# A gated recurrence and a feed-forward block on one core: chunk steps get explicit places, and some work changes engines

## The chip, the core and the metric

The kernel runs on one core of a Trainium2 chip. A core has a matrix engine (TensorE, PE in the profile, with PEld for its weight loads), a vector engine (DVE), an activation engine (ScalarE, ACT), GpSimd (POOL) and a queue of DMA issues (SyncE, SP). Each engine works through its own instructions strictly in the order in which they stand; semaphores tell one engine that another is done. The metric is the device time of one execution in microseconds; less is better. All tensors that the engines work on are fp32; the two weight matrices arrive as fp64.

## The reference

```python
batch, n_heads, seq, head_dim = (4, 8, 768, 48)          # q, k, v, a_re, a_im
n_tokens, d_model, d_ff = (3072, 384, 2048)              # w_in (384, 2048), w_out (2048, 384)
mag = np.sqrt(a_re * a_re + a_im * a_im)
scale = np.minimum(mag, 0.999) / (mag + 1e-06)
a_re_n, a_im_n = (a_re * scale, a_im * scale)
for t in range(S):                                       # state S is complex, 48 x 48 per head
    new_re = ar * S_re - ai * S_im
    new_im = ar * S_im + ai * S_re
    S_re, S_im = (new_re + kv, new_im)                   # kv = k_t (outer) v_t
    y[:, :, t] = np.einsum('bhd,bhde->bhe', q[:, :, t], S_re)
x = y.transpose(0, 2, 1, 3).reshape(B * S, H * D)        # (3072, 384)
h = x @ w_in
sp = np.maximum(h, 0.0) + np.log1p(np.exp(-np.abs(h)))
out = (h * erf(sp)) @ w_out
```

## The kernel before

The 3072 tokens are cut into 12 units of 256 tokens (three to a batch), and a unit into two chunks of 128 tokens. For a unit the kernel does four things.

- **Gates** (`g_tan`, `g_turn`, `g_angle`, `g_sin`, `g_log`, `g_decay`): magnitude and angle of the gates, summed along the chunk by a product with a triangular matrix (tile `sum`). The angle is the arc tangent of ai/ar, and 1/ar is a DVE reciprocal (lines 734 and 735, tile `rec`) of a clamped ar; lines 743 and 745 clamp the squared magnitude (`s`) and the quotient (`th`). They end in factors `pr` and `CS`.
- **Chunk** (`chunk`, twice a unit): q and k are multiplied by the factors on DVE (`kr`, `qr`, `kt`, `qt`), transposed on PE (`tr`) and copied out of PSUM by ACT (`kT`, `qT`, line 846). The scores `sc` are masked on DVE into `A` (line 857), the chunk's k-v products `kv` update the state `S`, and `y` is built on PE from `A` and `S`. ACT copies it to `x` (line 890), PE transposes that (`xt`), ACT copies it to `xT` (line 899).
- **Input product** (`ff_in`, line 914): `h` = x @ w_in in two slabs of 1024 columns, 96 PE instructions a unit, copied out by ACT (line 916). `softplus` clamps h on DVE into `z` (line 930) and then runs Exp, Ln, Ln and Exp over the slab on ACT: `z` is the softplus, `yy` its reciprocal. `erf_times_h` takes a slab in four parts: GpSimd multiplies z by yy into `t` (line 948), ACT runs Gelu over z in place, and DVE combines them (lines 949, 951 and 952) in place into h.
- **Output product** (`ff_out`, line 966): h @ w_out, 64 PE instructions a unit, copied out by ACT to `o` (line 970) and stored.

The fp64 weights are read as integers and converted (`narrow`, lines 683 to 693) in 14 pieces, six of w_in and eight of w_out. A piece is four DVE instructions, a GpSimd one, two DVE, a GpSimd one, all over one buffer `words`, which shares the tag `z` (one buffer) with softplus: the pieces run strictly one after the other, and the first softplus waits for the last piece.

The main loop has 16 windows. Window w runs the chunks of unit w, the input product of unit w-1, the output product of unit w-2 and gates of units w+1 to w+3. Inside a window `weave` gives each stream of steps an interval, spreads its steps evenly over it and issues them by that place; the 22 chunk steps run evenly from 0 to 1. From the issued order and its own estimate of durations a scheduler then fixes the order on each engine. `act` groups the activations by table (three table sets), and a change of set costs a table load (line 638).

After the loop the kernel sums two collected quantities, compares each with a bound, and takes a second, slower way of computing (`product_path`) if a bound is exceeded.

## Time and profile before

| | |
|---|---|
| time, median of 3 runs | 985.98 us (983.36 to 987.53) |
| the profiled execution's own time | 981.68 us |
| its span, first to last instruction | 980.0 us |
| mean granted TensorE clock | 0.922 |
| PE busy | 812.8 us, 83% |
| DVE busy | 632.6 us, 65% |
| ACT busy | 579.6 us, 59% |
| POOL busy | 309.4 us, 32% |

Busy time is a sum over the whole span, so a share such as 83% mixes a beginning in which PE has little to do with a middle in which it hardly pauses; the windows of the section below take these stages apart. The granted clock is given as a share of 2.4 GHz. A fp32 product is recorded as two matmul instructions, so counts of line 914 and 966 are twice those of the program's order.

### The profile page before, as it was taken

How to read it: one execution, taken by the hardware profiler on the slowest of the kernel's cores; microseconds unless marked ns; L12 is line 12 of the kernel's file. 1: busy time of each engine (PE TensorE's matmuls, PEld its weight loads, DVE VectorE, ACT ScalarE, POOL GpSimd, SP SyncE). 2: the span in 40 equal slices, each digit the busy share in tenths (PEclk: the TensorE clock that was granted, in tenths of full speed). 3: DMA queues.
4: the chain of work that ended last, by engine and by line, in shares of the span. 5: the costliest groups of instructions: out<-in, count | busy, mean ns of one | idle time of the engine just before them, and what ended most of it. 6: DMA issues, size and time to landing. Idle time of an engine off the chain costs nothing. (4 is left out here: it accounts for less than half of the span.)

```text
span 980.0 us, 10235 instructions
## 1 busy us (share of the span) xinstructions
PE 812.8 (83%) x3882; PEld 618.2 (63%) x3882; DVE 632.6 (65%) x736; ACT 579.6 (59%) x737; POOL 309.4 (32%) x180
## 2 busy tenths in 40 slices
PE   0115788968849989999999898998999999999987
PEld 0004677755637767777767676776767786887654
DVE  6778987638687576865975965767647534664340
ACT  4515241236777777758568587677684766556650
POOL 3565443324342242431431423224302220132220
PEclk9998575888978989999999999999999899999989
DMA  7552333101030211120311211111011110000000
GB/s 171 133 151 71 86 81 97 49 0 33 2 77 19 34 33 33 33 49 18 65 33 23 43 33 34 33 33 33 7 27 34 33 33 1 17 1 17 1 16 20
DMA packets 148034, 41.77 MB, mean 43 GB/s; under 512 B 142068, under 2 KB 145160, under 8 KB 147208
## 3 DMA queue, kind: packets, MB, share of 16 engines
q1 hardware_dynamic: 147976, 41.03, 18.4%
q8 instruction: 32, 0.52, 0.2%
q14 instruction: 26, 0.21, 0.1%
HBM read 36.24 MB, written 4.75 MB: 42 GB/s over the span
## 5 line engine op out<-in xcount | busy, mean ns | idle before, releaser
L966 PE MATMUL ops<-w_out_sb,h 128*128 128x384 f32 x768 | 286.0, 512 | 16.6 <-DVE h L952 8.9
L914 PE MATMUL hps<-xT,w_in_sb 128*128 128x256 f32 x1152 | 267.8, 387 | 16.9 <-ACT h L916 14.6
L914 PEld LDWEIGHTS hps<-xT,w_in_sb 128*128 128x128 f32 x1152 | 220.3, 194 | 59.0 <-ACT h L916 15.9
L948 POOL TENSOR_TENSOR t<-z,yy 128x512 f32<-128x512 f32 x96 | 148.0, 1560 | 301.0 <-ACT yy L639 261.3
L639 ACT ACTIVATE z<-z 128x2048 f32<-128x2048 f32 (+1 forms) x144 | 152.2, 1057 | 119.9 <-POOL t L948 84.8
L966 PEld LDWEIGHTS ops<-w_out_sb,h 128*128 128x128 f32 x768 | 146.3, 200 | 99.7 <-issue 16.9
L949 DVE SCALAR_TENSOR_TENSOR yy<-t,yy 128x512 f32<-128x512 f32 x96 | 101.6, 1083 | 74.0 <-POOL t L948 74.0
L916 ACT COPY h<-hps 128x512 f32<-128x512 f32 x96 | 55.5, 581 | 86.1 <-PE hps L914 85.4
L951 DVE TENSOR_TENSOR z<-z,yy 128x512 f32<-128x512 f32 x96 | 88.0, 946 | 0.0
L882 PE MATMUL y<-v,A 128*128 128x48 f32 x384 | 77.2, 298 | 11.5 <-DVE A L857 11.5
L857 DVE TENSOR_TENSOR A<-sc,triu 128x512 f32<-128x512 f32 x48 | 32.7, 684 | 79.4 <-PE sc L854 79.4
L638 ACT ACT_TABLE_LOAD x64 | 82.1, 1283 | 1.1
L854 PEld LDWEIGHTS sc<-qT,kT 96*128 96x128 f32 x384 | 54.6, 214 | 44.5 <-ACT qT L846 40.3
L930 DVE TENSOR_SCALAR z<-h 128x1024 f32<-128x1024 f32 x48 | 42.2, 887 | 62.1 <-ACT h L916 59.9
L854 PE MATMUL sc<-qT,kT 96*128 96x128 f32 x384 | 61.0, 308 | 24.4 <-ACT qT L846 23.8
L765 PE MATMUL sum<-th,turns 128*128 128x384 f32 x48 | 26.4, 637 | 65.7 <-DVE th L762 50.6
L952 DVE SCALAR_TENSOR_TENSOR h<-z,h 128x512 f32<-128x512 f32 x96 | 78.4, 846 | 0.1
L882 PEld LDWEIGHTS y<-v,A 128*128 128x128 f32 x384 | 65.1, 216 | 16.1 <-DVE A L857 12.9
L885 PE MATMUL y<-S,qT 96*128 96x48 f32 x320 | 69.3, 302 | 0.0
L793 POOL TENSOR_TENSOR lr<-s,y 128x768 f32<-128x768 f32 x12 | 24.9, 2078 | 127.1 <-ACT y L639 97.0
L735 DVE RECIPROCAL rec<-rec 128x768 f32<-128x768 f32 x12 | 59.4, 4950 | 0.3
L885 PEld LDWEIGHTS y<-S,qT 96*128 96x128 f32 x320 | 56.0, 218 | 0.0
(80 smaller groups left out, 972.4 us busy)
## 6 DMA issues: line engine op xcount, KB each, us to landing
raw<-in_moe_w_in_dram SPq DMA_DIRECT2D x6, 1024.0 KB, 7.1
raw<-in_moe_w_out_dram SPq DMA_DIRECT2D x8, 768.0 KB
ar<-in_a_re_dram SPq DMA_DIRECT2D x24, 192.0 KB, 3.2
ai<-in_a_im_dram SPq DMA_DIRECT2D x24, 192.0 KB, 3.4
q<-in_q_dram SPq DMA_DIRECT2D x24, 192.0 KB, 3.6
k<-in_k_dram SPq DMA_DIRECT2D x24, 192.0 KB, 2.9
v<-in_v_dram SPq DMA_DIRECT2D x24, 192.0 KB, 3.8
out_dram<-o SPq DMA_DIRECT2D x24, 192.0 KB, 1.9
```

Of the source, the lines that this page charges most:

```text
L638: in_order(nc.scalar.preload_act_table_set(sets[0]))
L639: in_order(nc.scalar.activation(func=func, **kw))
L735: nc.vector.reciprocal(out=rec, in_=rec)
L854: nc.tensor.matmul(out=ps[:, j, :], lhsT=st["k", g][0:D2, j, :], rhs=st["q", g][0:D2, j, :], start=True, stop=True)
L882: nc.tensor.matmul(out=y[:, j, :], lhsT=st["A", g][:, i, :], rhs=T["v", u][:, c, j, :], start=True, stop=first)
L885: nc.tensor.matmul(out=y[:, j, :], lhsT=st["q", g][0:D2, i, :], rhs=T["S"][0:D2, j, :], start=False, stop=True)
L914: nc.tensor.matmul(out=ps[:, e, :], lhsT=w_in_sb[:, kd, f0:f0 + P], rhs=T["xT", u][:, kd, :], start=(kd == 0), stop=(kd == KD - 1))
L948: nc.gpsimd.tensor_tensor(out=t, in0=z, in1=y, op=OP.mult)
L949: nc.vector.scalar_tensor_tensor(out=y, in0=t, scalar=-2.0, in1=y, op0=OP.add, op1=OP.mult)
L951: nc.vector.tensor_tensor(out=z, in0=z, in1=y, op=OP.mult)
L952: nc.vector.scalar_tensor_tensor(out=h, in0=z, scalar=1.0 / RT2, in1=h, op0=OP.add, op1=OP.mult)
L966: nc.tensor.matmul(out=ps, lhsT=T["h", u, sl][:, e, jj * P:(jj + 1) * P], rhs=w_out_sb[:, i, :], start=(i == 0), stop=(i == KF - 1))
```

## The change

- The chunk steps get places of their own in a window: a list of (place, step) with the 11 steps of a chunk between 0.0 and 0.45 of its half of the window, `state` before the scores, and both `qT` copies ahead of them. All streams are put in one list `plan` and sorted. The gate steps of a unit move: `g_mag` and `g_log` of unit w+2, `g_angle`, `g_decay` and `g_sin` of unit w+1, where the angles were those of w+2 and the magnitudes those of w+3.
- The clamps and the reciprocal go. 1/ar becomes Ln and Exp on ACT (in `g_log`), the softplus reads h directly. In their place five sums are collected, partly as by-products of activations (`accum_out`), and compared with five bounds (`LIMITS`; the last is for the sum of the reciprocals `yy`) at the end.
- Gelu writes a buffer `e` of its own (two of them), where it wrote over z. The product t = z * yy goes from GpSimd to DVE.
- The copies `qT`, `x` and `o` go from ACT to DVE.

```diff
+LIMITS = (1e13, 0.0, 1e15, 1e18, 1e8)
...
-    def g_tan(u):
+    def g_mag(u):
...
-            act(out=m, in_=m, func=AF.Relu, accum_out=off[:, u:u + 1])
-            T["s"], T["y"] = s, y
+            T["s"], T["y"], T["m"] = s, y, m

         def s1():
-            rec = t_("rec")
-            nc.vector.tensor_scalar(out=rec, in0=ar, scalar1=2.0**-60, scalar2=None, op0=OP.max)
-            nc.vector.reciprocal(out=rec, in_=rec)
-            T["rec"] = rec
-
-        def s2():
-            rec = T["rec"]
-            nc.gpsimd.tensor_tensor(out=rec, in0=rec, in1=ai, op=OP.mult)
-
-            s = T["s"]
-            nc.vector.tensor_scalar(out=s, in0=s, scalar1=2.0**-63, scalar2=2.0**63, op0=OP.max, op1=OP.min)
-            th = gat.tile([P, C, DM], FP, tag="th", name="th")
-            nc.vector.tensor_scalar(out=th.rearrange("p c f -> p (c f)"), in0=rec, scalar1=SLOPE, scalar2=-SLOPE,
-                                    op0=OP.min, op1=OP.max)
-            T["th", u] = th
-        return [s0, s1, s2]
+            act(out=T["m"], in_=T["m"], func=AF.Relu, bias=LEAST, accum_out=off[:, u:u + 1])
+        return [s0, s1]
...
     def g_log(u):
...
+            act(out=m, in_=ar, func=AF.Ln)
+            act(out=m, in_=m, func=AF.Exp, scale=-1.0)
             act(out=s, in_=s, func=AF.Ln)
             act(out=y, in_=s, func=AF.Exp, scale=-0.5)
             act(out=y, in_=y, func=AF.Ln, scale=EPS, bias=1.0)
+            th = gat.tile([P, C, DM], FP, tag="th", name="th")
+            nc.gpsimd.tensor_tensor(out=th.rearrange("p c f -> p (c f)"), in0=m, in1=ai, op=OP.mult)
...
-                nc.scalar.copy(out=t[0:D2], in_=ps[0:D2])
+                (nc.scalar.copy if nm == "k" else nc.vector.tensor_copy)(out=t[0:D2], in_=ps[0:D2])
...
-            nc.scalar.copy(out=x, in_=y.rearrange("p h d -> p (h d)"))
+            nc.vector.tensor_copy(out=x, in_=y.rearrange("p h d -> p (h d)"))
...
-        return [prep("k", 1), prep("q", 0), cols("k", 0), cols("k", 1), cols("q", 0), scores(0), cols("q", 1),
-                scores(1), state, y_, xT]
+        return [(0.0, prep("k", 1)), (0.03, prep("q", 0)), (0.06, cols("k", 0)), (0.09, cols("k", 1)),
+                (0.12, cols("q", 0)), (0.15, cols("q", 1)), (0.2, state), (0.25, scores(0)), (0.28, scores(1)),
+                (0.36, y_), (0.45, xT)]
...
     def softplus(u, sl):
...
-            for i in range(0, SLAB, half):
-                nc.vector.tensor_scalar(out=z[:, i:i + half], in0=h[:, i:i + half], scalar1=8.0, scalar2=-16.0,
-                                        op0=OP.min, op1=OP.max)
-            act(out=z, in_=z, func=AF.Exp)
+            act(out=z, in_=T["h", u, sl], func=AF.Exp, accum_out=exps[:, i:i + 1])
...
-                nc.gpsimd.tensor_tensor(out=t, in0=z, in1=y, op=OP.mult)
+                e = yp.tile([P, n, NT], FP, tag="e", name="e", bufs=2)
+                act(out=e, in_=z, func=AF.Gelu, scale=RT2)
+                nc.vector.tensor_tensor(out=t, in0=z, in1=y, op=OP.mult)
                 nc.vector.scalar_tensor_tensor(out=y, in0=t, scalar=-2.0, in1=y, op0=OP.add, op1=OP.mult)
-                act(out=z, in_=z, func=AF.Gelu, scale=RT2)
-                nc.vector.tensor_tensor(out=z, in0=z, in1=y, op=OP.mult)
-                nc.vector.scalar_tensor_tensor(out=h, in0=z, scalar=1.0 / RT2, in1=h, op0=OP.add, op1=OP.mult)
+                nc.vector.tensor_tensor(out=e, in0=e, in1=y, op=OP.mult)
+                nc.vector.scalar_tensor_tensor(out=h, in0=e, scalar=1.0 / RT2, in1=h, op0=OP.add, op1=OP.mult)
...
-                    nc.scalar.mul(out=o, in_=ps, mul=-RT2)
+                    nc.vector.tensor_scalar(out=o, in0=ps, scalar1=-RT2, scalar2=None, op0=OP.mult)
...
-            (0.0, 1.0, rec),
...
-            (0.0, 0.45, f0), (0.45, 0.9, f1),
...
+            plan += [(0.5 * c + p, f) for c in range(C) for p, f in chunk(w, c)]
+        plan += at(0.0, 0.9, weights_in() if w == -1 else weights_out() if w == 0 else [])
+        plan += at(0.0, 1.0, only(w - 2, ff_out))
...
+        for _, f in sorted(plan, key=lambda e: e[0]):
+            f()
```

The first place is DVE in the beginning, where pieces of w_out are converted (`words`, `w_out_sb`) among the chunks of the second unit (numbers tell buffers apart). Line numbers after are those of the changed kernel. Before:

```order
L735 RECIPROCAL rec_960<-rec_960 128x768
L683 TENSOR_SCALAR words_440<-raw_439 128x768
L792 TENSOR_SCALAR s_552<-s_552 128x768
L684 TENSOR_SCALAR words_440<-words_440 128x768
L874 TENSOR_TENSOR Skv_855<-kv_845,S_664 96x384
L685 TENSOR_SCALAR words_440<-raw_439 128x768
L857 TENSOR_TENSOR A_810<-sc_805,triu_114 128x512
L687 SCALAR_TENSOR_TENSOR w_out_sb_128<-raw_439,words_440 128x768
L875 TENSOR_TENSOR S_854<-Skv_855,w_412 96x384
L857 TENSOR_TENSOR A_837<-sc_832,triu_114 128x512
```

After:

```order
L686 TENSOR_SCALAR words_433<-raw_432 128x768
L868 TENSOR_TENSOR S_742<-Skv_743,w_449 96x384
L687 TENSOR_SCALAR words_433<-words_433 128x768
L850 TENSOR_TENSOR A_759<-sc_754,triu_114 128x512
L688 TENSOR_SCALAR words_433<-raw_432 128x768
L850 TENSOR_TENSOR A_774<-sc_769,triu_114 128x512
L690 SCALAR_TENSOR_TENSOR w_out_sb_131<-raw_432,words_433 128x768
L883 COPY x_814<-y_797 128x384
L693 TENSOR_SCALAR words_433<-w_out_sb_131 128x768
```

The reciprocal is gone from between the conversion's instructions; the copy of `x`, which waits for PE's `y`, now stands between them.

The second place is DVE in a unit in the middle, at the second half of a slab's elementwise work (the same instructions for the first half stand just ahead). Before:

```order
L949 SCALAR_TENSOR_TENSOR yy<-t,yy 128x512 x2
L951 TENSOR_TENSOR z<-z,yy 128x512 x2
L952 SCALAR_TENSOR_TENSOR h<-z,h 128x512 x2
L762 SCALAR_TENSOR_TENSOR th<-row,th 1x384
L930 TENSOR_SCALAR z<-h 128x1024
L743 TENSOR_SCALAR s<-s 128x768
```

After:

```order
L937 TENSOR_TENSOR t<-z,yy 128x512 x2
L938 SCALAR_TENSOR_TENSOR yy<-t,yy 128x512 x2
L939 TENSOR_TENSOR e<-e,yy 128x512 x2
L940 SCALAR_TENSOR_TENSOR h<-e,h 128x512 x2
L824 TENSOR_TENSOR qr<-q,pr 128x384
L839 COPY qT<-tr 96x512 x2
L850 TENSOR_TENSOR A<-sc,triu 128x512 x2
L958 TENSOR_SCALAR o<-ops 128x384
```

Before, DVE went on with clamps and angles, since ACT made `qT`. Now the two `qT` copies of the second chunk stand in DVE's queue, behind the 16 elementwise instructions of a slab, of which four are the products `t`.

The third place is PE for the same chunk, from the transposes of q to `y`. Before:

```order
L843 MATMUL tr<-ident,qt 96x128 x4
L966 MATMUL ops<-w_out_sb,h 128x384 x4
L854 MATMUL sc<-qT,kT 128x128 x4
L843 MATMUL tr<-ident,qt 96x128 x4
L966 MATMUL ops<-w_out_sb,h 128x384 x2
L854 MATMUL sc<-qT,kT 128x128 x4
L966 MATMUL ops<-w_out_sb,h 128x384 x2
L866 MATMUL kv<-v,kt 96x48 x8
```

After:

```order
L908 MATMUL hps<-xT,w_in_sb 128x256 x6
L836 MATMUL tr<-ident,qt 96x128 x8
L908 MATMUL hps<-xT,w_in_sb 128x256 x6
L954 MATMUL ops<-w_out_sb,h 128x384 x4
L859 MATMUL kv<-v,kt 96x48 x8
L847 MATMUL sc<-qT,kT 128x128 x8
L954 MATMUL ops<-w_out_sb,h 128x384 x4
```

Between the transposes of q and the scores, which need the `qT` copies, there stood 4 and 2 output products; now there stand 6 input products, 4 output products and the 8 products `kv`.

## Rows read from the trace of the kernel before

**Rows 1.** The page: engines over the span; granted TensorE clock in 40 slices.
```profile
PE 812.8 (83%) x3882; PEld 618.2 (63%) x3882; DVE 632.6 (65%) x736; ACT 579.6 (59%) x737; POOL 309.4 (32%) x180
...
PEclk9998575888978989999999999999999899999989
```

**Rows 2.** Windows: stretch, length, then PE, PEld, DVE, ACT, POOL busy (count), clock, DMA.
```profile
0.00:212.00 212.00, 120.34 (x512) 96.38 (x512) 160.24 (x170) 70.01 (x109) 95.62 (x53) 0.82 0.38 97
212.00:314.00 102.00, 72.41 (x288) 51.72 (x289) 71.15 (x77) 73.92 (x84) 38.38 (x23) 0.80 0.16 31
314.00:902.00 588.00, 554.48 (x2862) 426.20 (x2862) 376.43 (x456) 405.31 (x514) 164.69 (x96) 0.98 0.14 29
902.00:980.00 78.00, 65.58 (x222) 43.88 (x222) 24.74 (x36) 30.38 (x31) 10.71 (x8) 0.91 0.04 14
```

**Rows 3.** Windows of line 914 alone: PE and PEld busy (count), clock, DMA.
```profile
314.00:902.00 588.00, 199.57 (x865) 162.82 (x866) 0.98 0.14 29
```

**Rows 4.** Windows, one late stretch (columns as in rows 2).
```profile
842.00:902.00 60.00, 59.47 (x313) 46.17 (x314) 32.66 (x45) 35.99 (x42) 12.74 (x8) 1.00 0.02 8
```

**Rows 5.** Waits of PE from 314 to 902 us: total, times, longest.
```profile
PE xt L898 <- ACT x L890: 11.2, 8, 2.7
PE sc L854 <- ACT qT L846: 8.4, 10, 1.7
```

**Rows 6.** Timeline (start us, us, instruction): first and last weight conversion begin, what follows.
```profile
31.57 0.68 DVE L683 TENSOR_SCALAR words<-raw 128x1024 uint32<-128x1024 uint32 x1
...
203.58 0.56 DVE L683 TENSOR_SCALAR words<-raw 128x768 uint32<-128x768 uint32 x1 [1.99 <-POOL w_out_sb L693]
...
211.78 1.29 DVE L930 TENSOR_SCALAR z<-h 128x1024 f32<-128x1024 f32 x2 [1.98 <-POOL w_out_sb L693]
```

**Rows 7.** Lines of DVE, 31.5 to 212 us: count | busy, mean ns | idle.
```profile
L735 DVE RECIPROCAL rec<-rec 128x768 f32<-128x768 f32 x3 | 14.8, 4944 | 0.0
...
L745 DVE TENSOR_SCALAR th<-rec 128x768 f32<-128x768 f32 x4 | 7.4, 1858 | 0.0
...
L743 DVE TENSOR_SCALAR s<-s 128x768 f32<-128x768 f32 x3 | 7.1, 2378 | 8.2 <-POOL s L726 8.2
```

**Rows 8.** Timeline: second A tile of a chunk, the copy of its y.
```profile
145.44 0.68 DVE L857 TENSOR_TENSOR A<-sc,triu 128x512 f32<-128x512 f32 x1
...
151.34 0.48 ACT L890 COPY x<-y 128x384 f32<-128x384 f32 x1 [9.75 <-PE y L885]
```

**Rows 9.** Lines over the whole span (columns as in rows 7).
```profile
L948 POOL TENSOR_TENSOR t<-z,yy 128x512 f32<-128x512 f32 x96 | 148.0, 1560 | 301.0 <-ACT yy L639 261.3 <-DVE Skv L874 24.6 <-DVE yy L949 15.1
...
L949 DVE SCALAR_TENSOR_TENSOR yy<-t,yy 128x512 f32<-128x512 f32 x96 | 101.6, 1083 | 74.0 <-POOL t L948 74.0
...
L638 ACT ACT_TABLE_LOAD x64 | 82.1, 1283 | 1.1
...
L639 ACT ACTIVATE yy<-z 128x2048 f32<-128x2048 f32 x24 | 45.9, 1911 | 0.3
L930 DVE TENSOR_SCALAR z<-h 128x1024 f32<-128x1024 f32 x48 | 42.2, 887 | 62.1 <-ACT h L916 59.9 <-POOL w_out_sb L693 2.0
...
L857 DVE TENSOR_TENSOR A<-sc,triu 128x512 f32<-128x512 f32 x48 | 32.7, 684 | 79.4 <-PE sc L854 79.4
...
L639 ACT ACTIVATE y<-s 128x768 f32<-128x768 f32 x12 | 10.2, 854 | 0.1
```

**Rows 10.** Lines of ACT by form: the Gelu.
```profile
L639 ACT ACTIVATE z<-z 128x512 f32<-128x512 f32 x96 | 60.5, 630 | 86.7 <-POOL t L948 84.8
```

**Rows 11.** Timeline: line 949 with no GpSimd work beside it.
```profile
289.68 0.68 DVE L949 SCALAR_TENSOR_TENSOR yy<-t,yy 128x512 f32<-128x512 f32 x1
```

**Rows 12.** Timeline of PE: input products back to back.
```profile
785.67 2.75 PE L914 MATMUL hps<-xT,w_in_sb 128*128 128x256 f32 x12
```

**Rows 13.** Timeline: the last two groups of output products.
```profile
935.79 10.48 PE L966 MATMUL ops<-w_out_sb,h 128*128 128x384 f32 x32
...
951.05 23.40 PE L966 MATMUL ops<-w_out_sb,h 128*128 128x384 f32 x64 [4.65 <-ACT o L970]
```

More of the change, by code (lines that the diff above doesn't have):

```diff
@@ L624, in quotient_path @@
     nc.vector.tensor_scalar(out=turns, in0=triu, scalar1=1.0 / TAU, scalar2=None, op0=OP.mult)
-    off = const.tile([P, NU], FP, name="off")
-    spans = const.tile([P, NU * C], FP, name="spans")
+    seen = [const.tile([P, n], FP, name=f"seen{i}") for i, n in enumerate((NU * C, NU, NU, NU * NSL, NU * NSL))]
+    spans, off, large, exps, inverse = seen
     w_in_sb = const.tile([P, KD, FF], FP, name="w_in_sb")
@@ L978, in only, with at @@
         return steps(u) if 0 <= u < NU else []
+    def at(begin, end, steps):
+        return [(begin + (end - begin) * (i + 0.5) / len(steps), f) for i, f in enumerate(steps)]
     load_gates(0)
-    load_gates(1)
     load_qkv(0)
-    for f in g_tan(0):
-        f()
     for w in range(-2, NU + 2):
-        load_gates(w + 4)
+        load_gates(w + 3)
         if w >= -1:
             load_qkv(w + 2)
-        rec = chunk(w, 0) + chunk(w, 1) if 0 <= w < NU else []
-        f0 = only(w - 1, lambda u: ff_in(u, 0) + softplus(u, 0) + erf_times_h(u, 0))
-        f1 = only(w - 1, lambda u: ff_in(u, 1) + softplus(u, 1) + erf_times_h(u, 1))
-        wts = weights_in() if w == -1 else weights_out() if w == 0 else []
-        weave(
-            (0.0, 1.0, rec),
-            (0.0, 0.05, only(w + 2, g_turn) + only(w + 1, g_sin)),
-            (0.0, 0.9, wts),
-            (0.0, 0.45, f0), (0.45, 0.9, f1),
-            (0.2, 1.0, only(w - 2, ff_out)),
-            (0.3, 0.7, only(w + 2, g_angle)),
-            (0.15, 0.151, only(w + 1, g_decay) + only(w + 2, g_log)),
-            (0.5, 0.8, only(w + 3, g_tan)),
-        )
@@ L1005, in quotient_path @@
-    total = const.tile([P, 2], FP, name="total")
-    nc.vector.tensor_reduce(out=total[:, 0:1], in_=spans, axis=mybir.AxisListType.X, op=OP.add)
-    nc.vector.tensor_reduce(out=total[:, 1:2], in_=off, axis=mybir.AxisListType.X, op=OP.add)
-    ps = ps_b.tile([P, 2], FP, tag="b", name="all")
-    nc.tensor.matmul(out=ps[0:1, :], lhsT=ones, rhs=total, start=True, stop=True)
-    both = const.tile([1, 2], FP, name="both")
-    nc.vector.tensor_scalar(out=both[:, 0:1], in0=ps[0:1, 0:1], scalar1=SPAN, scalar2=None, op0=OP.is_le)
@@ L1012, in quotient_path @@
-    nc.vector.tensor_scalar(out=both[:, 1:2], in0=ps[0:1, 1:2], scalar1=0.0, scalar2=None, op0=OP.is_le)
-    nc.vector.tensor_tensor(out=ok, in0=both[:, 0:1], in1=both[:, 1:2], op=OP.mult)
+        plan = []
+        if 0 <= w < NU:
+            plan += [(0.5 * c + p, f) for c in range(C) for p, f in chunk(w, c)]
+        plan += at(0.0, 0.9, weights_in() if w == -1 else weights_out() if w == 0 else [])
+        plan += at(0.0, 1.0, only(w - 2, ff_out))
+        if 0 <= w - 1 < NU:
+            for sl in range(NSL):
+                b = 0.06 + 0.4 * sl
+                plan += at(b, b + 0.24, ff_in(w - 1, sl))
+                plan += [(b + 0.25, softplus(w - 1, sl))]
+                plan += at(b + 0.3, b + 0.42, erf_times_h(w - 1, sl))
@@ new lines, in quotient_path @@
+        plan += at(0.05, 0.1, only(w + 2, g_mag))
+        plan += at(0.1, 0.45, only(w + 1, g_angle))
+        plan += at(0.3, 0.305, only(w + 1, g_decay))
+        plan += at(0.71, 0.711, only(w + 2, g_log))
+        plan += at(0.9, 0.95, only(w + 1, g_sin) + only(w + 2, g_turn))
+        for _, f in sorted(plan, key=lambda e: e[0]):
+            f()
+    n = len(seen)
+    sums = const.tile([P, n], FP, name="sums")
+    for i, t in enumerate(seen):
+        nc.vector.tensor_reduce(out=sums[:, i:i + 1], in_=t, axis=mybir.AxisListType.X, op=OP.add)
@@ L1016 @@
+    ps = ps_b.tile([P, n], FP, tag="b", name="all")
+    nc.tensor.matmul(out=ps[0:1, :], lhsT=ones, rhs=sums, start=True, stop=True)
+    within = const.tile([1, n], FP, name="within")
+    for i, limit in enumerate(LIMITS):
+        nc.vector.tensor_scalar(out=within[:, i:i + 1], in0=ps[0:1, i:i + 1], scalar1=limit, scalar2=None, op0=OP.is_le)
+    nc.vector.tensor_reduce(out=ok, in_=within, axis=mybir.AxisListType.X, op=OP.min)
 def kernel(
```

18 lines of the change are left out of this document (9 added, 9 removed).

## Prediction

> **What bounds the kernel now.** I read the page first. PE is busy 83% of the span, twenty per cent ahead of the next engine, but the line of its granted clock falls below full speed almost only in the first third [rows 1]. So one share for the whole span says little, and I cut the span into four stages by events of the program [rows 2]: to 212 us, where the last weight conversion ends; to 314, where the input product of the third unit begins; to 902, where that of the twelfth begins; and to the end. Line 914 alone has 865 instructions between 314 and 902, nine units of 96 [rows 3], so a unit takes 588 / 9 = 65.3 us there.
>
> In these nine units PE is busy 554.5 of 588 us at a clock of 0.98 [rows 2], and between 842 and 902, where the gates are all done and DVE, ACT and POOL have least to do, 59.5 of 60.0 us [rows 4]. That is PE's own pace: 60 us a unit. The 5.3 us above it are the price of being fed late; the waits that end last are copies by ACT, 11.2 us for `x` and 8.4 us for `qT` [rows 5].
>
> Before 212 us PE does 120 us of work at a clock of 0.82. The stage is set by the 14 weight conversions, which run from 31.57 to 211.78 us, one after the other over one buffer, alternating between DVE and POOL; directly behind the last stands the first clamp of softplus [rows 6]. The last piece, with nothing between its instructions, takes 211.78 - 203.58 = 8.2 us; the mean is 180.2 / 14 = 12.9. The rest is what stands in DVE's queue between them. From 212 to 314 PE is busy 72 of 102 us, since the first output product waits for the first slab's softplus and the third unit's chunks for ACT and DVE. After 902 it is busy 65.6 of 78 us [rows 2].
>
> **The change part by part.** Sums are made against the profiled execution: a span of 980.0 us and 1.7 us around it, 981.7, which is 4.3 us below the median of the three runs, 985.98.
>
> *Beginning.* Between the first and the last conversion DVE loses three reciprocals, 14.8 us, four clamps of the angle, 7.4 us, and three of the magnitude, 7.1 us: 29.3 us [rows 7]. It gains, for the four chunks of the first two units, eight `qT` copies and four `x` copies. DVE's copy out of PSUM is not in the trace; the nearest row is the mask `A`, which reads as many columns out of PSUM, 0.68 us, against 0.48 us for ACT's copy of `x` [rows 8]. I take 0.68: 12 x 0.68 = 8.2 us. And DVE now waits for PE: `x` stands one or two conversion instructions behind the second `A`. Before, from the end of that `A` (146.1) to the copy of `x` (151.3) 5.2 us passed [rows 8], of which the two conversion instructions between take about 1.2 [rows 6]. Three chunks (the very first has half the products and its `x` stands far behind) make 3 x 4 = 12 us. What is queued behind the waiting copy is the conversion itself, so this is on the path. Against that, four instructions of the third unit's first chunk (two of them `A`) now stand behind the last conversion: 4 x 0.7 = 3 us less. Sum: -29.3 + 8.2 + 12 - 3 = -12. Bounds: -29 if PE is always early, +6 if each `qT` also waits 2 us.
>
> *Filling up.* After the last conversion ACT sets the pace, since a slab's four passes take 4 x 1.91 = 7.6 us [rows 9]. Before, each slab also had clamps ahead of it and the Gelu wrote over z, so it had to wait for POOL's t: 84.8 us of waiting in all [rows 10]. Now a slab is 7.6 + two table loads of 1.28 + four Gelu of 0.63 + two copies of `h` at the Gelu's 0.6 + some 2.5 us for the two `e` buffers = 16.4 us; the second slab has five gate activations of 0.85 besides, 20.7. With Abs and Sin the third unit's factors are there 39 us after the last conversion. Its first chunk takes some 12 us; the second chunk's `qT` stands behind the next slab on DVE, whose Gelu ACT reaches 22 us later (about ten gate activations and four copies, then 7.6 and a load), at 61; DVE's 16 instructions at 0.68 [rows 11] end at 70, and `qT`, `A`, `y`, `x` and the transposes need 8 more. So the third unit's input product begins 78 to 80 us after the last conversion, instead of 102: -22. Bounds: -35, and 0 if DVE and ACT hold each other up as before.
>
> *The nine units.* PE's instructions stay the same, so 60 us is the floor. What fed it late changes: `qT` and `x` go to DVE; behind the transposes of q PE now has six input products, four output products and `kv` to do instead of two to four output products. DVE's load was 376 / 9 = 41.8 us a unit [rows 2]. It loses the reciprocal and its clamps (about 7 us), four softplus clamps of 0.89 and, with POOL's t gone, the stretching of line 949 from 0.68 [rows 11] to 1.08 [rows 9], eight times: -14. It gains eight t and eight copies at 0.68: +10.9. So some 39 of 60. ACT had 405 / 9 = 45 us; it loses eight copies of 0.48 [rows 8] and gains two gate activations of 0.85 and six read-outs of sums, which I bound by the same 0.85 each: 43 to 48. Both stay under PE, which hides the read-outs and the copies; if that cover goes, they cost their 5 us a unit. I take half of the excess as won: 9 x 1.8 = -16. Bounds: 9 x 5.3 = -48 by the late stretch [rows 4], and above zero by the rival below.
>
> *Tail.* Before, 32 output products ran after the last input product, then PE waited 4.65 us and ran 64 [rows 13]. Now 44 products of the program's order, 88 instructions, follow the last input product, and the last slab's softplus lies beside the first 56 of them: 56 x 0.33 = 18 us against 7.6 + 1.3 + 0.6 for ACT and 5.4 for half a slab on DVE. So the 4.65 us go, and of the slack in 23.4 - 64 x 0.33 = 2.3 us part: with the clamps (2 x 0.89) gone -10 is my value, for the stage as a whole has 12.4 us without PE. Bounds: -12 and +2, the latter for the five comparisons at the end, which now wait for the last product.
>
> Sum: -12 - 22 - 16 - 10 = -60. 981.7 - 60 = 921.7; with the 4.3 us to the median, 926.
>
> **The rivals.** *Copies behind the elementwise block (slower).* In the nine units and the two before, DVE works through 16 instructions of a slab ahead of the second chunk's `qT`. They take 16 x 0.68 = 10.9 us, or 17.3 at the mean of 1.08 [rows 9]. Behind the transposes PE has 12 instructions of 0.23 [rows 12], 8 of 0.33 [rows 13] and `kv`, about 6.7 us. If DVE begins the block only when PE comes to those transposes, PE waits 5 to 11 us a unit. From 5.5 us on, 11 units eat the 60 us; at 8 the time is 926 + 88 = 1014. For it: strict order, and the block itself waits for ACT's Gelu. Against it: DVE has 20 us a unit to spare, and PE comes to the transposes only after that slab's input products.
>
> *PE is the bound and only the beginning moves.* Units and tail stay as they are: 926 + 26 = 952; if the fill does not move either, 974. For it: PE's work is unchanged and its waits in rows 5 are only 20 us. Against it: the late stretch at 60.
>
> *PE is fed without a gap.* All of 48 and the fill's 35: 926 - 32 - 13 = 881.
>
> *Headroom in PE.* By the share of weight loads, 46.2 of 60 us in the late stretch [rows 4], a unit could come down to 46 us, and nine of them would be 174 us shorter than now: about 800. But 96 x 0.23 + 64 x 0.33 = 43 us of a unit are the two big products back to back [rows 12, 13], and the chunks' products come on top, so the trace speaks against it. The Trainium skill's page "Perfetto Trace Analysis", section "Identifying the Most-Contended Engine", calls matmul busy time a bad measure of how near PE is to its limit and asks for the weight loads' share instead; by that rule this case would hold, and the row disagrees.
>
> *The condition fails.* Then the second path runs as well, and the time far exceeds 1500. With the reference's inputs the sum of the reciprocals is 9.1e6 against a bound of 1e8, and the others are further off.
>
> **How the numbers follow.** My forecast, 900 to 948: 0.52. Only the beginning moves, 948 to 981: 0.19. PE without a gap, 870 to 900: 0.08. Headroom: 0.01. Nothing to be seen, 981 to 991: 0.06. Copies behind the block, above 991: 0.135. The condition: 0.005. The runs before lie within 0.4%, so 0.5% is what can be told from no change. Faster: 0.52 + 0.19 + 0.08 + 0.01 = 0.80; same 0.06; slower 0.14. The range 882 to 985 leaves out about 0.05 below and 0.17 above; the likeliest case's own is 900 to 948.
>
> **What would show it.** Right: the last conversion ends near 200 us, the third unit's input product begins near 280, nine units take about 571 us, and 68 follow; DVE's mean for the line of `yy` falls to about 0.7; PE's longest wait for a DVE copy stays under 3 us. Wrong: conversions that end after 212 with DVE waiting for PE ahead of `x`; waits of PE's scores for `qT` of over 5 us in every unit; or a unit that still takes 65 us with PE waiting for ACT's copies of `h`.

## The result and the profile after

The changed kernel takes 896.94 us (median of 4 runs, 895.91 to 899.13) against 984.67 us before (977.97 to 987.53): a ratio of 0.912, 95% interval 0.907 to 0.917. That is 88 us less, where 60 were forecast (926 us); the time lies inside the range of 882 to 985, and just below the likeliest case's own range of 900 to 948.

The page of the changed kernel, engines over the span of 894.5 us and the granted clock in 40 slices (answers to [rows 1]):

```profile
PE 780.3 (87%) x3882; PEld 605.7 (68%) x3882; DVE 549.8 (61%) x838; ACT 559.4 (63%) x725; POOL 154.8 (17%) x84
...
PEclk9655685689999999999999999999999999999999
```

POOL has lost half of its work and DVE 83 us, though DVE has 102 instructions more. The same four stages, cut at the events of [rows 2]: end of the last conversion (192.8), third unit's input product (269.7), twelfth unit's (828.6). Columns as there.

```profile
0.00:192.80 192.80, 103.88 (x460) 85.89 (x460) 111.67 (x152) 59.37 (x94) 88.18 (x50) 0.69 0.39 103
192.80:269.70 76.90, 66.91 (x314) 48.42 (x314) 51.82 (x79) 66.61 (x80) 7.68 (x5) 0.96 0.15 30
269.70:828.60 558.90, 551.69 (x2898) 431.52 (x2897) 362.59 (x562) 404.94 (x521) 58.95 (x30) 0.99 0.16 33
828.60:894.50 65.90, 57.83 (x213) 39.86 (x212) 23.73 (x47) 28.52 (x31) 0.00 (x0) 0.97 0.05 17
```

The beginning is 19 us shorter than before, the fill 25, the nine units 29, the tail 12. In the nine units PE was busy about as long as before (551.7 against 554.5 us); what shrank is the time in which it did nothing, from 588.0 - 554.5 = 33.5 us [rows 2] to 558.9 - 551.7 = 7.2. In the fill, too, 20 of the 25 us are such time (29.6 us before, 10.0 now); the other 5 are PE's busy time, at a granted clock of 0.96 where it had been 0.80. The waits of PE in the nine units (total, times, longest) are these, and the copies `x` and `qT` of [rows 5] are no longer among them:

```profile
PE tr L836 <- DVE kt L828: 4.0, 6, 1.8
PE ops L954 <- DVE o L958: 2.7, 5, 1.0
PE y L875 <- ACT pr L642: 0.4, 1, 0.4
```

The elementwise lines over the whole span (count | busy, mean ns | idle, releaser), to be read beside [rows 9] and [rows 10]:

```profile
L938 DVE SCALAR_TENSOR_TENSOR yy<-t,yy 128x512 f32<-128x512 f32 x96 | 78.5, 851 | 0.0
L937 DVE TENSOR_TENSOR t<-z,yy 128x512 f32<-128x512 f32 x96 | 75.3, 818 | 50.4 <-ACT yy L642 50.4
L939 DVE TENSOR_TENSOR e<-e,yy 128x512 f32<-128x512 f32 x96 | 61.8, 682 | 0.8
L642 ACT ACTIVATE e<-z 128x512 f32<-128x512 f32 x96 | 57.0, 626 | 44.0 <-DVE h L940 43.7
```

The mean of `yy` fell from 1083 to 851 ns, not to the 0.7 us of the forecast, and the line waits for nothing; ACT's Gelu waits 44 us where it waited 86.7.

Where the beginning ends, in the timeline (start, us, instruction): one of the waits of the copy `x` for PE between conversions, the last conversion instructions of DVE and POOL, and the first elementwise work behind them.

```profile
163.90 0.56 DVE L883 COPY x<-y 128x384 f32<-128x384 f32 x1 [4.73 <-PE y L878]
...
189.94 0.96 DVE L694 SCALAR_TENSOR_TENSOR words<-raw,words 128x768 f32<-128x768 uint32 x1
...
191.04 1.80 POOL L696 TENSOR_TENSOR w_out_sb<-w_out_sb,words 128x768 f32<-128x768 f32 x1 [1.73 <-DVE words L694]
...
201.51 1.29 DVE L937 TENSOR_TENSOR t<-z,yy 128x512 f32<-128x512 f32 x2 [10.61 <-ACT yy L642]
```

### The profile page after: what moved, and what is told of

The parts are those of the page before. It is cut to its first block, busy times and chain, and to the rows that moved or that the text cites. A ratio compares the mean times of both kernels' runs of the same rounds, so it can differ in the third digit from the quotient of the medians.

```text
span 894.5 us, 10220 instructions
## 1 busy us (share of the span) xinstructions
PE 780.3 (87%) x3882; PEld 605.7 (68%) x3882; DVE 549.8 (61%) x838; ACT 559.4 (63%) x725; POOL 154.8 (17%) x84
## 4 chain that ended last, share of the span: by engine, by line
PE 55%; DVE 6%; ACT 3%; issue 2%
PE ops L954 20%; PE hps L908 19%; PE tr L836 4%; PE sc L847 3%; PE y L875 3%; DVE t L937 2%; PE y L878 2%; PE kv L859 2%; DVE yy L938 1%; PE sum L753 1%; PE sum L798 1%; ACT m L642 1%; ACT e L642 1%; DVE e L939 1%; DVE o L958 1%
## 5 line engine op out<-in xcount | busy, mean ns | idle before, releaser
L954 PE MATMUL ops<-w_out_sb,h 128*128 128x384 f32 x768 | 270.6, 495 | 6.8 <-DVE h L940 4.1
L937 DVE TENSOR_TENSOR t<-z,yy 128x512 f32<-128x512 f32 x96 | 75.3, 818 | 50.4 <-ACT yy L642 50.4
L784 POOL TENSOR_TENSOR th<-m,ai 128x768 f32<-128x768 f32 x12 | 24.4, 2036 | 349.0 <-ACT m L642 227.4
L642 ACT ACTIVATE e<-z 128x512 f32<-128x512 f32 x96 | 57.0, 626 | 44.0 <-DVE h L940 43.7
L938 DVE SCALAR_TENSOR_TENSOR yy<-t,yy 128x512 f32<-128x512 f32 x96 | 78.5, 851 | 0.0
L939 DVE TENSOR_TENSOR e<-e,yy 128x512 f32<-128x512 f32 x96 | 61.8, 682 | 0.8
L940 DVE SCALAR_TENSOR_TENSOR h<-e,h 128x512 f32<-128x512 f32 x96 | 61.7, 681 | 0.0
L847 PE MATMUL sc<-qT,kT 96*128 96x128 f32 x384 | 52.9, 290 | 7.5 <-DVE qT L839 6.5
L883 DVE COPY x<-y 128x384 f32<-128x384 f32 x24 | 13.3, 553 | 65.5 <-PE y L878 52.7
L836 PE MATMUL tr<-ident,kt 128*96 128x128 f32 x192 | 30.1, 298 | 25.2 <-DVE kt L828 25.2
```

The source lines that it names most:

```text
L642: in_order(nc.scalar.activation(func=func, **kw))
L836: nc.tensor.transpose(out=ps[0:D2, j, :], in_=st[nm][:, g * HG + j].rearrange("p u d -> p (u d)"), identity=ident)
L847: nc.tensor.matmul(out=ps[:, j, :], lhsT=st["k", g][0:D2, j, :], rhs=st["q", g][0:D2, j, :], start=True, stop=True)
L937: nc.vector.tensor_tensor(out=t, in0=z, in1=y, op=OP.mult)
L938: nc.vector.scalar_tensor_tensor(out=y, in0=t, scalar=-2.0, in1=y, op0=OP.add, op1=OP.mult)
L939: nc.vector.tensor_tensor(out=e, in0=e, in1=y, op=OP.mult)
```

## The experiments

Each kernel is the changed one with the edit shown, unless it says that it is the kernel before. All stages are cut at the same events; "ends" is the end of the last conversion, and the times of the stages are in us. Ratios are to the kernel before, run on the same chip, with 95% intervals. Every experiment was expected with two theories, A and B, and is measured against them.

| kernel | ends | fill | nine units | tail | span | median | ratio |
|---|---|---|---|---|---|---|---|
| before | 211.7 | 102.3 | 587.8 | 78.1 | 980.0 | 984.67 | 1 |
| changed | 192.8 | 76.9 | 558.8 | 65.9 | 894.5 | 896.94 | 0.912 (0.907-0.917) |
| copies_act | 186.5 | 80.5 | 549.8 | 67.4 | 884.2 | 888.24 | 0.900 (0.894-0.906) |
| t_pool | 194.4 | 87.8 | 584.4 | 68.9 | 935.4 | 939.08 | 0.952 (0.945-0.958) |
| gelu_in_place | 192.7 | 79.4 | 556.8 | 65.8 | 894.7 | 896.87 | 0.909 (0.903-0.916) |
| places_even | 187.7 | 89.8 | 563.9 | 63.0 | 904.3 | 906.06 | 0.920 (0.913-0.926) |
| recip_back | 210.4 | 87.6 | 540.9 | 66.0 | 904.8 | 909.35 | 0.924 (0.919-0.930) |
| clamp_back | 191.1 | 87.8 | 557.0 | 68.5 | 904.5 | 909.57 | 0.925 (0.919-0.930) |
| two_words | 165.5 | 102.8 | 557.4 | 65.7 | 891.4 | 895.52 | 0.912 (0.905-0.918) |
| before_copies_dve | 209.9 | 95.0 | 627.6 | 73.0 | 1005.5 | 1006.17 | 1.019 (1.011-1.027) |
| before_t_dve | 211.4 | 88.5 | 574.4 | 69.3 | 943.6 | 945.76 | 0.963 (0.961-0.964) |
| own_words | 201.5 | 43.1 | 558.7 | 68.5 | 871.8 | 872.82 | 0.887 (0.883-0.890) |
| recip_late | 201.1 | 78.1 | 546.8 | 65.7 | 891.7 | 895.86 | 0.909 (0.904-0.914) |
| own_words_rl | 204.1 | 46.8 | 552.3 | 67.9 | 871.1 | 870.33 | 0.883 (0.880-0.887) |

**t_pool: the product `t` back on GpSimd.**

```diff
-                nc.vector.tensor_tensor(out=t, in0=z, in1=y, op=OP.mult)
+                nc.gpsimd.tensor_tensor(out=t, in0=z, in1=y, op=OP.mult)
```

> The changed kernel with t = z*yy given back to GpSimd (Gelu keeps its own buffer). Theory A: DVE's line of yy goes back from 0.85 to 1.1 us or more and the chain in the fill gets longer (1.56 instead of 0.68 us a part), but PE covers it in the nine units: fill 77 to 82-90 us, nine units 559-565, total 903-915. Theory B (GpSimd beside DVE was what fed PE late): nine units 575 or more, total 920-940.

Theory B held. Nearly all of what the nine units had won is gone again (584.4), with 11 us of the fill and 3 of the tail. PE is busy for 551.6 us as in the changed kernel, so the 26 us are time in which it does nothing. The nine units (columns of [rows 2]; then waits of DVE and of PE there):

```profile
282.20:866.60 584.40, 551.58 (x2888) 432.34 (x2887) 351.11 (x480) 401.65 (x517) 163.27 (x104) 0.98 0.15 31
```

```profile
DVE yy L938 <- POOL t L937: 40.5, 32, 4.8
...
PE tr L836 <- DVE kt L828: 19.1, 9, 3.2
PE tr L836 <- ACT kT L839: 5.7, 6, 1.3
PE ops L954 <- DVE o L958: 5.4, 4, 1.6
```

DVE stands 40.5 us for `t`, and whatever is queued behind it on DVE (`kt`, `o`) comes late for PE. DVE is busy for only 351 of 584 us there, so it does not lack time; what is late is what stands behind the wait. Besides, the mean of `yy` there rises from 852 to 1189 ns (the last section tells why), and no run separates that from the wait.

**before_t_dve: the same edit alone, in the kernel before.** The edit is the diff above read backwards.

> The kernel before (985 us) with only t = z*yy moved from GpSimd to DVE; Gelu still writes over z, the order and the clamps stay. Theory A (GpSimd's product, which DVE and ACT wait for and which stalls DVE beside it, is worth its price by itself, as its undoing cost 42 us in the changed kernel): nine units 588 to 560-572, fill 102 to 88-96, total 945-962. Theory B (it only counts once the copies stand on DVE behind that block): nine units 580-590, total 970-983.

Total and fill came out as by theory A, the nine units between the two (574.4). The move pays without the rest, 37 us of the 88. PE's idle time in the nine units falls from 33.5 to 15.9 us, while its busy time rises by 4, at a granted clock of 0.96 instead of 0.98. The stretch, PE's waits in it, and the lines of DVE there that had 987 and 1041 ns before:

```profile
299.90:874.30 574.40, 558.46 (x2862) 438.49 (x2860) 368.45 (x539) 403.94 (x521) 65.11 (x25) 0.96 0.14 29
```

```profile
PE sc L854 <- ACT qT L846: 15.1, 8, 3.3
PE sum L765 <- DVE th L762: 0.5, 1, 0.5
```

```profile
L951 DVE TENSOR_TENSOR z<-z,yy 128x512 f32<-128x512 f32 x72 | 48.1, 703 | 28.6 <-ACT z L639 28.4
...
L949 DVE SCALAR_TENSOR_TENSOR yy<-t,yy 128x512 f32<-128x512 f32 x72 | 46.3, 683 | 0.0
```

The wait for `x`, the largest in [rows 5], is gone although ACT still copies `x`. It had been an effect of `t`: in the kernel before, ACT had waited for POOL's `t` just ahead of the copy, at each of the eight waits. One of them in the timeline, ACT and then PE:

```profile
543.82 0.63 ACT L639 ACTIVATE z<-z 128x512 f32<-128x512 f32 x1 [1.04 <-POOL t L948]
544.36 0.46 ACT L890 COPY x<-y 128x384 f32<-128x384 f32 x1
...
544.87 0.55 PE L898 MATMUL xt<-ident,x 128*128 128x128 f32 x3 [2.71 <-ACT x L890]
```

The wait for `qT` has another origin. It grows from 8.4 to 15.1 us when `t` moves, and in the kernel before, in eight of its ten cases, ACT had waited 1.0 to 2.5 us for DVE's clamp of h shortly before the copy. No run takes the clamp alone out of the kernel before, so that its removal ends this wait is read from the trace and not shown.

```profile
595.95 1.91 ACT L639 ACTIVATE z<-z 128x2048 f32<-128x2048 f32 x1 [1.51 <-DVE z L930]
597.76 0.56 ACT L846 COPY qT<-tr 96x512 f32<-96x512 f32 x1
```

**copies_act: `qT`, `x` and `o` back on ACT.**

```diff
-                (nc.scalar.copy if nm == "k" else nc.vector.tensor_copy)(out=t[0:D2], in_=ps[0:D2])
+                nc.scalar.copy(out=t[0:D2], in_=ps[0:D2])
...
-            nc.vector.tensor_copy(out=x, in_=y.rearrange("p h d -> p (h d)"))
+            nc.scalar.copy(out=x, in_=y.rearrange("p h d -> p (h d)"))
...
-                    nc.vector.tensor_scalar(out=o, in0=ps, scalar1=-RT2, scalar2=None, op0=OP.mult)
+                    nc.scalar.mul(out=o, in_=ps, mul=-RT2)
```

> The changed kernel (897 us) with the copies qT, x and o given back to ACT, all else as changed. Theory A (the copies on ACT were what fed PE late): DVE no longer waits for PE between conversions, so the last conversion ends some 14 us earlier (its waits for y are 13.8 us), but the nine units from the third input product to the twelfth grow from 559 to 570-580 us with PE waiting for ACT ahead of sc and xt; total 895-905. Theory B (the places and the work off ACT did it, the copies' engine does not matter): the nine units stay at 555-562, only the beginning gets shorter, total 880-888.

Theory B held for the time, and the nine units came out below it: 549.8, 9 us less than with the copies on DVE. The conversions end 6 us earlier, not 14. DVE no longer waits 13.8 us for `y`, but it waits longer for POOL's part of the conversions (36 us instead of 33) and for other products of PE (0.9 us for `whole` and none for `Skv` in the changed kernel):

```profile
DVE whole L758 <- PE sum L753: 5.7, 3, 2.7
DVE Skv L867 <- PE kv L859: 5.1, 2, 2.6
```

The nine units:

```profile
267.00:816.80 549.80, 546.39 (x2885) 429.41 (x2884) 313.70 (x488) 431.61 (x592) 58.37 (x30) 0.99 0.17 34
```

PE idles 3.4 us instead of 7.2 with ACT busy for 431.6 of 549.8 us: ACT had the room. Some 4 of the 9 us are work that falls outside of the window (558 output products in it by the trace, 570 in the changed kernel, at 0.33 us [rows 13]); the rest is pace. In all, this part of the change costs about 9 us.

**before_copies_dve: the copies alone on DVE, in the kernel before.**

> The kernel before (985 us) with only the three copies qT, x and o moved to DVE. Theory A (without the new places the copies stand behind the elementwise block and the reciprocal): PE waits for qT and x by 3 to 8 us a unit more, and conversions wait for y; slower, 1000-1050. Theory B (ACT's copies were what fed PE late, whatever the order): nine units 588 to 570-580, total 965-980.

Theory A held for the total: it is 1 to 3% slower, and the nine units grow by 40 us to 627.6. But this is not the mechanism of the prediction's slower rival. Only 14 of the 40 us are idle time of PE (47.5 instead of 33.5); the other 26 are its busy time, 580.1 instead of 554.5 us. Some 5 of these are work that falls into the window (566 output products by the trace instead of 552); the rest goes with a granted clock of 0.93 instead of 0.98. Whether the waits brought the lower clock no run shows. The stretch and PE's waits there:

```profile
304.90:932.50 627.60, 580.11 (x2880) 448.21 (x2878) 433.56 (x539) 384.21 (x451) 165.58 (x101) 0.93 0.13 27
```

```profile
PE sum L765 <- DVE th L762: 21.7, 5, 5.5
PE xt L898 <- DVE x L890: 7.1, 2, 6.9
PE sc L854 <- DVE qT L846: 6.5, 4, 3.9
PE y L882 <- DVE A L857: 4.4, 2, 3.1
```

PE waits for `qT` 6.5 us in all, where the rival and theory A had it in every unit. The largest wait is for `th` of the angles, which had cost 5.6 us before: with more on DVE, what it had done nearly in time comes late.

**places_even: the chunk's eleven steps in the old order, spread evenly.**

```diff
-        return [(0.0, prep("k", 1)), (0.03, prep("q", 0)), (0.06, cols("k", 0)), (0.09, cols("k", 1)),
-                (0.12, cols("q", 0)), (0.15, cols("q", 1)), (0.2, state), (0.25, scores(0)), (0.28, scores(1)),
-                (0.36, y_), (0.45, xT)]
+        steps = [prep("k", 1), prep("q", 0), cols("k", 0), cols("k", 1), cols("q", 0), scores(0), cols("q", 1),
+                 scores(1), state, y_, xT]
+        return [(0.5 * (i + 0.5) / len(steps), f) for i, f in enumerate(steps)]
```

> The changed kernel with the eleven steps of a chunk back in their old order (first scores between the two q transposes, the state products behind the scores) and spread evenly over the half window; the copies stay on DVE. Theory A (copies behind the elementwise block, which the new places cover): PE waits for the copy qT ahead of its scores by 2 to 6 us a unit, nine units 580-610, total 920-950. Theory B (the places are worth nothing by themselves): nine units 555-565, total 892-905.

The time of 906 us lies between the two, nearly at theory B's end, and the interval of its ratio overlaps that of the changed kernel. The nine units are 5 us longer, but PE idles 5.7 us in them instead of 7.2, and by the trace 14 output products more fall into the window (584 against 570, at 0.33 us [rows 13]), so no price of the places shows there. PE waits 3.7 us in all for `x` and not at all for `qT`. The difference lies ahead of them: the input product of the first unit begins at 140 us instead of 116, of the second at 201 instead of 184, of the third at 277 instead of 270. With the copies on DVE and the old order of steps the nine units take 564 us here and 628 in before_copies_dve; so the new places alone are not what covers the copies. What else differs between the two is `t`, the clamps, the reciprocal, Gelu's buffer, the windows of the gate steps and the granted clock (0.98 and 0.93).

**gelu_in_place: Gelu over `z` again, behind `t`.** The two instructions behind it then read and write `z` in place of `e`.

```diff
-                act(out=e, in_=z, func=AF.Gelu, scale=RT2)
...
+                act(out=z, in_=z, func=AF.Gelu, scale=RT2)
```

> The changed kernel with Gelu writing over z again, so that it stands behind t, which stays on DVE. Theory A: ACT waits for DVE's t ahead of each Gelu, which shows in the fill and the tail alone: +3 to +8 us there, nine units within 4 us of 559, total 900-908. Theory B (ACT is held up by it in every unit and PE with it): nine units 572 or more, total 912-930.

Neither theory's time: there is no difference, 896.87 against 896.94 us; the fill is 2.5 us longer and the nine units 2 shorter. Gelu must wait for `t` again, but with `t` on DVE this costs nothing. So the buffer by itself has no price; that the long wait of [rows 10] was for a `t` made on POOL is what before_t_dve and t_pool bear out.

**recip_back and recip_late: the reciprocal.** The first puts reciprocal and gate clamps back on DVE for all units, the second the reciprocal alone, from the fourth unit on.

```diff
-            act(out=m, in_=ar, func=AF.Ln)
-            act(out=m, in_=m, func=AF.Exp, scale=-1.0)
+            nc.vector.tensor_scalar(out=m, in0=ar, scalar1=2.0**-60, scalar2=None, op0=OP.max)
+            nc.vector.reciprocal(out=m, in_=m)
+            nc.vector.tensor_scalar(out=s, in0=s, scalar1=2.0**-63, scalar2=2.0**63, op0=OP.max, op1=OP.min)
...
+            nc.gpsimd.tensor_tensor(out=m, in0=m, in1=ai, op=OP.mult)
+            nc.vector.tensor_scalar(out=th.rearrange("p c f -> p (c f)"), in0=m, scalar1=SLOPE, scalar2=-SLOPE,
+                                    op0=OP.min, op1=OP.max)
```

> The changed kernel with the reciprocal of ar and the clamps of magnitude and angle back on DVE in place of Ln and Exp on ACT (the sums stay). Theory A (DVE's queue between the conversion instructions sets the beginning): about 3 reciprocals of 4.9 us, 3 or 4 angle clamps of 1.9 and as many magnitude clamps of about 0.7 to 2.4 come back before the last conversion, so it ends 15-25 us later; the rest is unchanged; total 912-922. Theory B (the conversions hide them): the last conversion moves by less than 5 us, total 895-903.

Theory A held for the beginning: the last conversion ends at 210.4, 17.6 us later. The rest did not stay as it was: the fill grows by 11 us as well, and the nine units take 540.9 us, the shortest of all, so the total rises by 12 only. In them PE is never idle, at 60.1 us a unit:

```profile
298.00:838.90 540.90, 540.90 (x2883) 428.24 (x2881) 388.54 (x573) 381.29 (x490) 53.42 (x28) 0.99 0.16 33
```

Of these 18 us 7 are idle time of the changed kernel, and some 5 are work outside the window by the trace (8 output products and 8 transposes fewer, at about 0.3 us).

```diff
-            act(out=m, in_=ar, func=AF.Ln)
-            act(out=m, in_=m, func=AF.Exp, scale=-1.0)
+            if u < 3:
+                act(out=m, in_=ar, func=AF.Ln)
+                act(out=m, in_=m, func=AF.Exp, scale=-1.0)
+            else:
+                nc.vector.reciprocal(out=m, in_=ar)
```

> The changed kernel with 1/ar from the fourth unit on by DVE's reciprocal (without clamps), as Ln and Exp on ACT only for the first three units, whose gates lie beside the weight conversions. Theory A (behind the beginning ACT has less room than DVE, so the 541 us of the nine units with the reciprocal back were ACT's two activations gone): beginning and fill as in the changed kernel (193, 270), nine units 543-552 instead of 559, total 880-891. Theory B (the 541 us came from the late start alone, with more work ready for PE by then): nine units 556-562, total 894-900.

Theory A held in the nine units: 546.8 instead of 558.8. Its total of 880 to 891 was missed. The time stays at 896 us, because the conversions end 8 us later; the fourth unit's reciprocal still found its way between them:

```profile
123.42 4.93 DVE L782 RECIPROCAL m<-ar 128x768 f32<-128x768 f32 x1
```

The nine units:

```profile
279.20:826.00 546.80, 543.57 (x2897) 430.05 (x2896) 388.93 (x569) 392.65 (x504) 54.86 (x29) 1.00 0.16 33
```

In the nine units PE does the same work in both (570 output products). Four of the 12 us are its idle time (7.2 and 3.2 us), the other eight its busy time, at a granted clock of 1.00 instead of 0.99. So taking the reciprocal and its clamps off DVE is worth nearly 18 us in the beginning, and up to 12 are lost in the nine units, where ACT has two activations more in every unit. It is up to 12, since the start at 279 instead of 270 us gave ACT and DVE a lead, and no run takes that apart. That ACT's two activations are the cause is not shown either. In the changed kernel PE waits there for DVE's `kt` and `o`; but `kt` had waited for ACT's `CS`, in the changed kernel three times as long as here, and this speaks for ACT. First the changed kernel, then recip_late:

```profile
DVE kt L828 <- ACT CS L642: 14.6, 8, 1.8
...
DVE kt L831 <- ACT CS L642: 4.8, 8, 1.8
```

**clamp_back: the clamp of h ahead of each softplus.**

```diff
-            act(out=z, in_=T["h", u, sl], func=AF.Exp, accum_out=exps[:, i:i + 1])
+            h, half = T["h", u, sl], SLAB // 2
+            for j in range(0, SLAB, half):
+                nc.vector.tensor_scalar(out=z[:, j:j + half], in0=h[:, j:j + half], scalar1=8.0, scalar2=-16.0,
+                                        op0=OP.min, op1=OP.max)
+            act(out=z, in_=z, func=AF.Exp, accum_out=exps[:, i:i + 1])
```

> The changed kernel with the clamp of h to [-16, 8] back on DVE ahead of each softplus (two instructions a slab). Theory A: one pass more in the chain of each slab, which only the fill shows: +2 to +4 us; nine units within 4 us of 559; total 898-903. Theory B (the clamps, queued on DVE behind other work, held ACT up in every unit): nine units 570 or more, total 908 or more.

Neither theory held: the nine units stay (557.0), but the fill grows by 11 us. These lines show ACT's wait for the clamp in the window of the fill, and the clamp of the second slab in DVE's queue, behind the first slab's elementwise work:

```profile
ACT z L642 <- DVE z L921: 17.4, 3, 8.5
```

```profile
212.16 0.68 DVE L944 SCALAR_TENSOR_TENSOR h<-e,h 128x512 f32<-128x512 f32 x1
212.76 1.29 DVE L921 TENSOR_SCALAR z<-h 128x1024 f32<-128x1024 f32 x2
```

**two_words: two buffers for the conversions by turns.**

```diff
-        tmps = zp.tile([P, 2, n], U32, tag="z", name="words")
+        T["piece"] = T.get("piece", -1) + 1
+        pool, tag = ((zp, "z"), (yp, "yy"))[T["piece"] % 2]
+        tmps = pool.tile([P, 2, n], U32, tag=tag, name="words")
```

> The changed kernel with the conversion's temporary taken by turns from the buffer z and from the buffer yy, which is idle until the first softplus, so that two pieces overlap. Theory A (the beginning is set by the chain DVE-GpSimd-DVE-GpSimd over one buffer): the last conversion ends 25-45 us earlier than 193 us, and the third unit's input product begins as much earlier less some 10 us of contention; total 860-885. Theory B (the beginning is set by DVE's total work, or by GpSimd and DVE slowing each other): the last conversion ends less than 12 us earlier; total 885-897.

The conversions do end 27 us earlier, as theory A has it, and nothing comes of it: 895.5 us. Pieces of w_out that are now ready sooner stand ahead of the first unit's second chunk, whose `kr` begins at 120.36 us instead of 88.59, so the second unit's input product begins at 208 instead of 184, and the third's at 268 instead of 270. First this run, then the same `kr` in the changed kernel:

```profile
118.46 1.98 DVE L689 TENSOR_SCALAR words<-words 128x768 f32<-128x768 uint32 x1
120.36 0.55 DVE L826 TENSOR_TENSOR kr<-k,pr 128x384 f32<-128x384 f32 x1
...
88.59 1.84 DVE L824 TENSOR_TENSOR kr<-k,pr 128x384 f32<-128x384 f32 x1
```

**own_words and own_words_rl: a faster version.** The copies are on ACT as in copies_act, Gelu writes over `z`, `t` has one buffer instead of two, and the conversions and their order change:

```diff
+    wp = ctx.enter_context(tc.tile_pool(name="wp", bufs=1))
...
-        tmps = zp.tile([P, 2, n], U32, tag="z", name="words")
+        T["piece"] = i = T.get("piece", -1) + 1
+        pool, tag = ((zp, "z"), (yp, "yy"))[i % 2] if i < 6 else (wp, "words")
+        tmps = pool.tile([P, 2, n], U32, tag=tag, name="words")
...
-        plan += at(0.0, 0.9, weights_in() if w == -1 else weights_out() if w == 0 else [])
+        plan += at(0.0, 0.9, weights_in() if w == -1 else weights_out()[:2] if w == 0 else weights_out()[2:] if w == 1 else [])
```

> A version meant to be faster: the changed kernel with the copies qT, x and o on ACT, Gelu over z (which cost nothing), the conversions of w_in by turns in the buffers z and yy, those of w_out in a buffer of their own, so that softplus need not wait for them, and six of these eight pieces a window later, behind the chunks of the first unit. Theory A (the beginning is set by the order of DVE's queue around the conversions, PE bounds the rest): the third unit's input product begins at 225-245 instead of 267 us, nine units 550-560, total 850-870. Theory B (DVE's total work sets the beginning, whatever its order): the third unit at 258 or later, total 875-888.

It takes 872.8 us. The third unit begins at 244.6, at the late edge of theory A, and the total misses its upper end by 3 us, below theory B's 875. The last conversion ends later than in the changed kernel (201.5), but softplus no longer waits for it, so that the first slabs' work lies beside the conversions. Its beginning and fill:

```profile
0.00:201.50 201.50, 109.22 (x532) 87.79 (x532) 151.43 (x173) 98.84 (x143) 95.41 (x52) 0.77 0.39 102
201.50:244.60 43.10, 41.14 (x235) 32.55 (x234) 23.89 (x36) 33.75 (x49) 3.99 (x3) 0.96 0.19 38
```

With the late reciprocal besides:

> The faster version (873 us: copies on ACT, own buffer for the conversions of w_out, six of its pieces a window later) with that late reciprocal too. Theory A: nine units 545-552 instead of 559, third unit at 245 as there, total 858-867. Theory B: no change, 870-876.

It takes 870.3 us, as by theory B: the nine units win 6 us, but the third unit begins 6 later. The two versions can't be told apart (0.883 to 0.890, 0.880 to 0.887); both are faster than the changed kernel.

## Why the prediction was right, and where it was off

*Beginning, -12 forecast, -19 measured.* The mechanism held: the reciprocal and the clamps left DVE's queue, and waits of `x` for PE's y came in, of which 3 x 4 us were forecast; the four copies waited 13.8 in all. That the sum came near is in part luck, since both large terms were taken too large and their errors cancel. Putting the reciprocal and the clamps back moves the last conversion by 17.6 us (recip_back), not by 29.3: DVE's waits for y shrink there from 13.8 to 7.2, so part of what comes back fills time in which DVE had stood. Taking the copies away moves it by 6 (copies_act), not by 8.2 + 12, since other waits take their place. What I had left out is that the first conversion also begins earlier, at 27.2 instead of 31.6 us.

*Fill, -22 forecast, -25 measured.* 78 to 80 us behind the last conversion were worked out, 76.9 measured. But the sum had several causes in it with no price each, and I had put the most on Gelu's buffer, by the 84.8 us of [rows 10]. gelu_in_place shows 2.5 us for that; t_pool, clamp_back and recip_back lengthen the fill by 11 each, places_even by 13. These prices are not pure: in each of the four the granted clock of the fill is 0.86 to 0.89 instead of 0.96, and the forecast had no term for the clock. The clamps' price is not their 0.9 us but their place behind sixteen instructions in DVE's queue.

*Nine units, -16 forecast, -29 measured.* Here the step failed that reads "I take half of the excess as won", and with it the reason given for it. I took ACT's copies for what fed PE late, by [rows 5], and `t` for mere load on DVE that PE covers. The runs show the reverse: the copies' move costs some 5 us there and 9 in all (copies_act), the reciprocal's removal up to 12 (recip_late), and `t` gives about 26 (t_pool). A wait list names the instruction that came last, not what had held up its engine: behind `x <- ACT` stood ACT's own wait for POOL's `t`, and behind most of `qT <- ACT` its wait for the clamp of h. The loads themselves came out as forecast, DVE 40.3 us a unit for 39 and ACT 45.0 for 43 to 48. The sum could have gone by the row that needed no half: PE's idle time there, 33.5 us [rows 2], of which 26 went.

*Tail, -10 forecast, -12 measured.* Right: the wait of 4.65 us [rows 13] is gone, and the last output products run back to back:

```profile
865.83 20.48 PE L954 MATMUL ops<-w_out_sb,h 128*128 128x384 f32 x63
```

*The rivals.* "Copies behind the elementwise block" did not come: with the copies on DVE PE waits 6.5 us in all for `qT` in the nine units of the old program and not at all in the new one, also with the old places (places_even). The old program did get slower by the copies, but through `th` and a lower granted clock. "Only the beginning moves" fell with the nine units. "Fed without a gap" came nearer than its 0.08: 7.2 us of idle PE are left. Headroom by the weight loads did not show: in recip_back PE is busy all through the nine units, with the weight loads at 428 of 540.9 us, and takes 60.1 us a unit, as [rows 4] had it; no run went below.

*What is not settled:* the undone parts (t 42, clamps 12, reciprocal 12, places 9, Gelu 0, copies -9) add up to 66 of 88 us. Every edit also lets the scheduler order the rest anew, and two parts were undone by no run: the gate steps' move to other windows, and the single sorted list of steps in place of `weave`. Whether the remaining 22 us are theirs stays open.

## What to carry to other kernels

Where an engine's copy comes late, look at what that engine itself waited for just before, and price that; moving the copy may only move the wait. In a strictly ordered queue an instruction costs what stands ahead of it, so the same edit can be worth -18 us where a queue is the bound and lose up to 12 where another engine is. And work moved between engines should be judged stage by stage: here the beginning was shorter with the reciprocal on ACT and the nine units with it on DVE, though the run that tried both (recip_late) did not get a shorter total.
